# Moving the key stores of later scans, and most loads of values and keys, from SyncE's queue to ScalarE's

## The chip, the cores and the metric

The kernel runs on one core of a Trainium2 chip. The metric is the device time of one execution in microseconds (us); lower is better. Engines are named as in the profile: PE is TensorE's matmul, PEld its weight load, DVE is VectorE, ACT is ScalarE, POOL is GpSimd, and SP is SyncE, which in this kernel issues every DMA. A DMA is issued by an instruction in an engine's queue, which waits there, in order, until what it needs is ready.

## What is computed

A gated linear attention with complex decay per channel (4 batches, 8 heads, 768 tokens, head dimension 48) is followed by a 2-D Fourier transform of the tokens and channels with a norm and two MLP blocks. Cut to what matters:

```python
for t in range(S):                                   # attention, per batch and head
    S_re, S_im = ar*S_re - ai*S_im + outer(k[t], v[t]), ar*S_im + ai*S_re
    y[t] = q[t] @ S_re
x = y as [4, 768, 384]
u = x + real(fft(fft(x, tokens), channels)); un = norm(u)
x = u + relu(un @ w_ch1) @ w_ch2                     # channels 384 -> 1536 -> 384
h = relu(x.T @ w_tok1) @ w_tok2                      # tokens 768 -> 256 -> 768
u = x + h.T
out = u + relu(u @ w_ch1') @ w_ch2'
```

## The kernel before, in words

**A chain and dense work for each batch.** The *chain* of a batch is `stage1` (attention) and `stage2` (the Fourier transform as matmuls, and the norm). The *dense work* is the MLPs: `dense1`/`mlp2` and at the end `mlp`, whose long groups of matmuls are L934 (first product, nine matmuls 128x384 into a PSUM tile `l`) and L956 (second product, also nine); ACT evicts the first product with L938 into `h` (for some batches also L944 into `full`), DVE makes the remainder L947 from it, and DVE adds the second product at L959. There are three `l` tiles in PSUM. The chain of batch b+1 is laid over the dense work of batch b: the matmuls of a chain have priority on PE and dense work fills the gaps. On ACT, DVE, POOL and SP the priorities are the other way round (dense 0, conversion of weights 5, chain 10). A scheduler turns these priorities and its own estimates into one fixed order for each engine, so that a changed instruction moves others as well.

**stage1** is a scan of each channel's decay in steps of three tokens, and then a loop over eight chunks of 96 tokens. Batch 0 has its own scan (`first_scan`, stores at L452). Batches 1 to 3 use `scan`: of each of 16 steps, `st_a` loads (L554, L558), `st_b` to `st_f` make the decays on ACT, DVE and POOL, `st_g` makes two tiles `y` on DVE (L634, L637; four buffers `y00`, `y10`, `y01`, `y11`, named by tile and by the step's parity) and stores one half of each to `kn` in DRAM (L638, L639), and `st_t` transposes the tile on PE (L650, tile `s`) and copies it on ACT into `qkt` (L653, L655, L656). In the profile these stores are `kn<-y`. The two `kn` arrays of batches b and b+1 alternate.

**The loop over chunks** needs for chunk c the values `V` (one load, L749) and the keys `Kn` (two loads, L752, from `kn`). Both have two buffers; the loads of chunk c+2 stand behind the matmuls that read those of chunk c (L776, L777 and for V also L810, L816). ACT evicts the chunk's result into `xT` (L818), and DVE carries a state `T` from chunk to chunk.

**Conversions.** The weights come as pairs of 32-bit words and are converted once, under batches 0 and 1: a load `cvt` (L185, 56 of them), ACT L191 and L192, DVE L194, POOL L196, DVE L199, ACT L205, POOL L206, and a store to `wscr` (L207). All later uses load `w<-wscr` (L283, 180 of them). All of these DMAs are on SP's queue, and a DMA that waits holds up those behind it:

```python
        def load(self):
            ...
            w = self.place(p, j, b)
            sp.dma_start(out=r32(w), in_=wscr[p][j])
```

Of the kernel before, what the change touches and what calls it, by code (L numbers as in the profile page):

```python
# [48 lines left out]
def with_ap(ap, offset, dims):  # L49
    return bass.AP(ap.tensor, ap.offset + offset, [list(ap.ap[0])] + [list(d) for d in dims])  # L50
# [3 lines left out]
def attn_fft_mixer_kernel(ctx: ExitStack, tc: tile.TileContext, aL, xL, vL, wL, qN, kN, vN, arN, aiN,  # L54
# [18 lines left out]
    ve, se, ge = Prio(nc.vector, "v"), Prio(nc.scalar, "v"), Prio(nc.gpsimd, "v")  # L73
    te, sp = Prio(nc.tensor, "pe"), Prio(nc.sync, "sp")
# [17 lines left out]
    def alloc(tag, shape, dt=F32, name=None):  # L92
        n = 1
        for x in shape[1:]:
            n *= x
        t = pool.tile([128, SIZE[tag]], dt, tag=tag, bufs=BUFS[tag], name=name or tag)
        return shaped(t[0:shape[0], 0:n], shape)
# [3 lines left out]
    def palloc(tag, shape):  # L101
        n = 1
        for s in shape[1:]:
            n *= s
        t = psum.tile([128, 512], F32, tag=tag, bufs=PSB[tag], name=tag)
        v = t[0:shape[0], 0:n]
        if len(shape) == 3:
            v = v.rearrange("p (a b) -> p a b", b=shape[2])
        return v
# [438 lines left out]
    def scan(b, t, knd, qk):  # L548
# [78 lines left out]
        def st_g(i):  # L627
            d = t[i]
            m, P, xx, s0 = d["m"], d["P"], d["xx"], d["s0"]
            y1, y2 = ybuf[0][i % 2], ybuf[1][i % 2]  # L630
            x1 = xx[:, :, 0, :].unsqueeze(2).to_broadcast([128, m, 2, 48])
            o1 = with_ap(y1, 0, [(128, m), (64, 2), (1, 48)])
            o2 = with_ap(y2, 0, [(128, m), (64, 2), (1, 48)])
            ve.tensor_tensor(out=o1, in0=x1, in1=P[:, 0:m, 0:2, :], op=ALU.mult)  # L634
            ve.tensor_tensor(out=xx[:, :, 1, :], in0=xx[:, :, 1, :], in1=P[:, 0:m, 2, :], op=ALU.mult)
            x2 = xx[:, :, 1, :].unsqueeze(2).to_broadcast([128, m, 2, 48])
            ve.tensor_tensor(out=o2, in0=x2, in1=P[:, 0:m, 0:2, :], op=ALU.mult)  # L637
            sp.dma_start(out=knd[0, :, s0:s0 + m, :], in_=y1[0:64, 0:m, :])  # L638
            sp.dma_start(out=knd[1, :, s0:s0 + m, :], in_=y2[64:128, 0:m, :])  # L639

        def st_t(i, k):
            if not qk:
                qk.append(alloc("qk", [112, 12288], name="qkt").rearrange("p (k g s) -> p k g s", k=2, g=64))
            qkt = qk[0]
            d = t[i]
            s0 = d["s0"]
            y = ybuf[k][i % 2]
            ps = palloc("s", [112, NT, 128])
            for j in range(NT):
                te.transpose(ps[:, j, :], y[:, j, 0:112], ident)  # L650
            src = ps.rearrange("p s (g c) -> p g c s", g=2)
            if k == 0:
                se.copy(out=with_ap(qkt, s0, [(64 * 96 + 48, 2), (96, 64), (1, NT)]), in_=src)  # L653
            else:
                se.copy(out=with_ap(qkt, 64 * 96 + 47 - s0, [(96, 64), (-1, NT)]), in_=src[:, 0])  # L655
                se.copy(out=qkt[:, 0, :, 48 + s0:48 + NT + s0], in_=src[:, 1])  # L656

        def st_end():

            ends = alloc("e", [128, 2, 3, 48], name="ends")  # L660
            for j, f in enumerate((t[15]["P"][:, NT - 1], t[16]["P"][:, 0])):
                se.copy(out=ends[:, j], in_=f)
            t[0]["ends"] = ends
            F = ends[:, 1]
            w = alloc("e", [128, 2, 48], name="len")
            ve.tensor_tensor(out=w, in0=F[:, 0:2], in1=F[:, 0:2], op=ALU.mult)
            ve.tensor_tensor(out=w[:, 0], in0=w[:, 0], in1=w[:, 1], op=ALU.add)
            ve.tensor_tensor(out=w[:, 0], in0=w[:, 0], in1=F[:, 2], op=ALU.mult)
            se.activation(out=w[:, 1], in_=w[:, 0], func=ACTF.Square, scale=-1.0, bias=ones, accum_out=chk[:, 0:1])
            ve.tensor_reduce(out=chk[:, 1:2], in_=F[:, 2], axis=mybir.AxisListType.X, op=ALU.add)  # L670
            ve.tensor_scalar(out=good, in0=chk[:, 1:2], scalar1=CHK_C, scalar2=None, op0=ALU.is_lt)
            ve.scalar_tensor_tensor(out=good, in0=chk[:, 0:1], scalar=CHK_B, in1=good, op0=ALU.is_lt, op1=ALU.mult)
# [19 lines left out]
        for i in range(NS):  # L692
            if i + ahead < NS:
                st_a(i + ahead)
            n = t[i]["n"]
            for j in range(5):
                if j == 2:
                    part2(i + 1)
                if j == 4:
                    part1(i + 2)  # L700
                if j < n:
                    st_f(i, j)
            if t[i]["m"]:
                st_g(i)
                st_t(i, 0)
                st_t(i, 1)
        st_end()

    def stage1(b):
        t = [dict() for _ in SL]  # L710
        knd = kn[b % 2]
        qk = []
        tops = free if b == 0 else []
        if b == 0:
            first_scan(t, knd, qk)
        else:
            scan(b, t, knd, qk)
# [28 lines left out]

        def ch_load(c):
            v = alloc("P", [96, 384], name="V")
            sp.dma_start(out=v, in_=vL[b, c])  # L749
            kt = alloc("A", [96, 8, 128], name="Kn")  # L750
            for hf in range(2):
                sp.dma_start(out=kt[48 * hf:48 * hf + 48],  # L752
                             in_=knd[hf].rearrange("(h c) s f -> c s h f", c=8)[c])
            st[c] = dict(v=v, kt=kt)

# [64 lines left out]
        if b == 0:  # L820
            tick(CF[0])
        st_g2()
        ch_load(0)
        ch_load(1)
        ch_sc(0, 0)
        ch_sc(0, 1)
        for c in range(8):
            if c < 7:
                ch_u(c)
                ch_sc(c + 1, 0)  # L830
                ch_sc(c + 1, 1)
            ch_y(c)
            if b == 0 and WC[c]:
                warm(WC[c], ident)
            st["T"] = st.get("Tn")
            if c < 6:
                ch_load(c + 2)
            if b == 0 and c < 7:
                rests[0], rests[1] = tops[c], st["yop"]
                tick(CF[c + 1], c == 5)  # L840
# [520 lines left out]
```

## Time and profile before

| | |
|---|---|
| time, median of 3 runs | 1092.18 us (1091.67 to 1096.09) |
| the profiled execution | 1093.5 us, of which the trace's span is 1091.7 |
| busy: PE, PEld, DVE, ACT, POOL | 978.8, 915.3, 769.3, 511.1, 417.9 us |
| mean granted clock of PE | 0.966 |
| scans (first to last store) of batches 1, 2, 3 | 194.5 to 340.6; 422 to 522; 603 to 722 us |
| loops over chunks of batches 0 to 3 | 77 to 136; 344 to 397; 524 to 578; 723 to 776 us |

Busy time is the time in which an engine executed something; issuing a DMA is not counted in it. The spans of scans and loops are read from the starts of the stores, loads and matmuls named above. The end of the chain of batch 3 lies at about 831 us; after 850 us only dense work is left.

### The profile page before, as it was taken

How to read it: one execution, taken by the hardware profiler on the slowest of the kernel's cores; microseconds unless marked ns; L12 is line 12 of the kernel's file. 1: busy time of each engine (PE TensorE's matmuls, PEld its weight loads, DVE VectorE, ACT ScalarE, POOL GpSimd, SP SyncE). 2: the span in 40 equal slices, each digit the busy share in tenths (PEclk: the TensorE clock that was granted, in tenths of full speed). 3: DMA queues.
4: the chain of work that ended last, by engine and by line, in shares of the span. 5: the costliest groups of instructions: out<-in, count | busy, mean ns of one | idle time of the engine just before them, and what ended most of it. 6: DMA issues, size and time to landing. Idle time of an engine off the chain costs nothing.

```text
span 1091.7 us, 21067 instructions
## 1 busy us (share of the span) xinstructions
PE 978.8 (90%) x7314; PEld 915.3 (84%) x7314; DVE 769.3 (70%) x2083; ACT 511.1 (47%) x1425; POOL 417.9 (38%) x541
## 2 busy tenths in 40 slices
PE   1567788999899988999998999999897999999997
PEld 0337766989788986899997899999787999999997
DVE  6988887999999678999658879974734433433332
ACT  6753446777875236877216556842224112121111
POOL 6625994673676454345336312424512002000000
PEclk9988896999999999899999999999998999999999
DMA  6238943776668563465575345665303434543432
GB/s 219 48 101 233 290 165 118 252 264 206 200 235 270 162 180 113 117 184 175 156 198 148 100 139 187 203 165 132 128 17 117 146 114 135 159 156 127 163 101 76
DMA packets 101537, 174.66 MB, mean 160 GB/s; under 512 B 11056, under 2 KB 61104, under 8 KB 100912
## 3 DMA queue, kind: packets, MB, share of 16 engines
q1 hardware_dynamic: 101424, 173.24, 51.5%
q8 instruction: 60, 0.98, 0.4%
q14 instruction: 53, 0.43, 0.1%
HBM read 133.88 MB, written 39.32 MB: 159 GB/s over the span
## 4 chain that ended last, share of the span: by engine, by line
PE 68%; DVE 16%; DMA 6%; POOL 4%; ACT 3%; issue 2%; SPq 0%; POOLq 0%; DVEq 0%; ACTq 0%
PE l L956 24%; PE l L934 23%; PE s L761 4%; DMA cvt<-wL 3%; PE s L650 2%; PE s L1047 2%; PE s L810 2%; DVE cvt L199 2%; DVE ws L1002 2%; PE s L1036 1%; PE s L816 1%; PE s L1161 1%; POOL cvt L196 1%; DVE ws L996 1%; PE s L1179 1%
## 5 line engine op out<-in xcount | busy, mean ns | idle before, releaser
L956 PE MATMUL l<-w,h 128*128 128x384 f32 x1728 | 326.5, 339 | 6.8 <-DVE h L947 4.0
L934 PE MATMUL l<-th,w 128*128 128x384 f32 x1152 | 316.0, 344 | 8.8 <-DVE h L947 4.3
L956 PEld LDWEIGHTS l<-w,h 128*128 128x128 f32 x1728 | 297.2, 188 | 11.1 <-DVE h L947 6.3
L934 PEld LDWEIGHTS l<-th,w 128*128 128x128 f32 x1152 | 213.1, 191 | 12.2 <-DVE h L947 6.1
L934 PE MATMUL l<-tl,w 128*128 128x384 f32 x576 | 196.3, 341 | 3.6 <-DVE tl L918 3.6
L938 ACT ACTIVATE h<-l 128x384 fp32r<-128x384 f32 x192 | 94.1, 490 | 213.2 <-PE l L934 212.7
L959 DVE TENSOR_TENSOR u<-u,l 128x384 f32<-128x384 f32 x192 | 105.3, 549 | 83.1 <-PE l L956 82.4
L947 DVE SCALAR_TENSOR_TENSOR h<-l,h 128x384 fp32r<-128x384 f32 x160 | 88.5, 553 | 91.0 <-ACT h L938 90.8
L934 PEld LDWEIGHTS l<-tl,w 128*128 128x128 f32 x576 | 110.3, 191 | 4.2 <-DVE tl L918 4.2
L196 POOL TENSOR_TENSOR cvt<-cvt 128x384 int32<-128x384 int32 x56 | 66.3, 1190 | 38.3 <-DVE cvt L194 7.3
L761 PE MATMUL s<-qkt 112*96 112x96 f32 x512 | 57.8, 263 | 11.0 <-DVE sc L768 11.0
L472 PE MATMUL s<-misc,y 128*112 128x128 f32 x96 | 22.2, 379 | 47.3 <-DVE y L450 44.5
L761 PEld LDWEIGHTS s<-qkt 112*96 112x96 f32 x512 | 51.8, 173 | 13.8 <-DVE sc L768 12.0
L472 PEld LDWEIGHTS s<-misc,y 128*112 128x112 f32 x96 | 14.8, 183 | 57.0 <-POOL tm L366 19.1
L1146 POOL TENSOR_TENSOR xl<-u,xh 128x384 fp32r<-128x384 f32 x18 | 17.9, 1005 | 107.1 <-ACT xh L1145 107.1
L206 POOL TENSOR_TENSOR w<-cvt,w 128x384 fp32r<-128x384 f32 x44 | 52.2, 1197 | 8.3 <-ACT w L205 8.0
L199 DVE SCALAR_TENSOR_TENSOR cvt<-cvt 128x384 int32<-128x384 int32 x56 | 45.9, 828 | 5.9 <-POOL cvt L196 5.8
L579 POOL TENSOR_TENSOR tm<-tm 128x144 f32<-128x144 f32 (+1 forms) x51 | 26.8, 526 | 58.9 <-ACT tm L578 58.6
L945 POOL TENSOR_TENSOR h<-full,h 128x384 fp32r<-128x384 f32 x32 | 33.8, 1057 | 37.2 <-ACT full L944 35.4
L623 DVE TENSOR_TENSOR p<-p,A 128x144 f32<-128x144 f32 x144 | 44.6, 310 | 2.1
L650 PE MATMUL s<-misc,y 128*112 128x128 f32 x288 | 45.2, 276 | 0.9 <-DVE y L634 0.3
L794 POOL TENSOR_TENSOR yc<-Aa,gm 48x384 f32<-48x384 f32 x18 | 21.0, 1164 | 62.4 <-DVE Aa L787 62.4
(232 smaller groups left out, 1940.8 us busy)
## 6 DMA issues: line engine op xcount, KB each, us to landing
w<-wscr SPq DMA_DIRECT2D x180, 384.0 KB, 3.4
cvt<-wL SPq DMA_DIRECT2D x56, 384.0 KB, 5.0
wscr<-w SPq DMA_DIRECT2D x44, 384.0 KB, 3.7
Kn<-kn SPq DMA_DIRECT2D x64, 192.0 KB, 3.7
kn<-y SPq DMA_DIRECT2D x96, 96.0 KB, 2.6
raw<-aL SPq DMA_DIRECT2D x48, 144.0 KB, 3.1
xx<-xL SPq DMA_DIRECT2D x48, 144.0 KB, 2.9
V<-vL SPq DMA_DIRECT2D x32, 144.0 KB, 3.2
```

What stands on the lines that cost most here:

```text
L196: x = ge.tensor_tensor(out=a, in0=a, in1=lo, op=ALU.add)
L199: rest(ve.scalar_tensor_tensor(out=a, in0=hi, scalar=-0x80000000, in1=a, op0=ALU.bitwise_and, op1=ALU.bitwise_or))
L206: ge.tensor_tensor(out=parts[:, 1, :], in0=a.bitcast(F32), in1=r32(parts[:, 0, :]), op=ALU.subtract)
L472: te.transpose(ps[:, j, :], y[:, j, 0:112], ident)
L623: ve.tensor_tensor(out=cur, in0=prev, in1=A[:, j, 0:3, :], op=ALU.mult)
L650: te.transpose(ps[:, j, :], y[:, j, 0:112], ident)
L761: te.matmul(out=ps[:, j, :], lhsT=K[:, hc, :], rhs=Q[:, hc, :])
L934: te.matmul(out=ps, lhsT=w1[:, wi, kt * 128:kt * 128 + 128], rhs=x[g][:, kt, :], start=(n == 0), stop=(n == 8))
L938: x = se.activation(out=hi, in_=ps, func=ACTF.Relu)
L947: ve.scalar_tensor_tensor(out=lo, in0=ps, scalar=0.0, in1=r32(hi), op0=ALU.max, op1=ALU.subtract)
L956: te.matmul(out=ps, lhsT=hs[m][:, hi, tt * 128:tt * 128 + 128], rhs=w2[:, wi, :], start=(n == 0), stop=(n == 8))
L959: ve.tensor_tensor(out=u[tt], in0=u[tt], in1=ps, op=ALU.add)
```

## The change

The two stores of a scan's step leave `st_g` and SP's queue; in `st_t` each is written behind the copies of its tile, on ACT's queue. Of the loads of `V` and `Kn` those of chunks 0 and 1 stay on SP; those of chunks 2 to 7 go to ACT's queue. This holds for all four batches, whereas the stores of batch 0's scan (L452) stay. So 96 stores, 24 loads of `V` and 48 of `Kn` change the queue; no byte more or less is moved.

```diff
@@ scan.st_g
             ve.tensor_tensor(out=o2, in0=x2, in1=P[:, 0:m, 0:2, :], op=ALU.mult)
-            sp.dma_start(out=knd[0, :, s0:s0 + m, :], in_=y1[0:64, 0:m, :])
-            sp.dma_start(out=knd[1, :, s0:s0 + m, :], in_=y2[64:128, 0:m, :])
@@ scan.st_t
                 se.copy(out=with_ap(qkt, 64 * 96 + 47 - s0, [(96, 64), (-1, NT)]), in_=src[:, 0])
                 se.copy(out=qkt[:, 0, :, 48 + s0:48 + NT + s0], in_=src[:, 1])
+            h = slice(64 * k, 64 * k + 64)
+            se.dma_start(out=knd[k, :, s0:s0 + d["m"], :], in_=y[h, 0:d["m"], :])
@@ ch_load
             v = alloc("P", [96, 384], name="V")
-            sp.dma_start(out=v, in_=vL[b, c])
+            q = se if c > 1 else sp
+            q.dma_start(out=v, in_=vL[b, c])
             kt = alloc("A", [96, 8, 128], name="Kn")
             for hf in range(2):
-                sp.dma_start(out=kt[48 * hf:48 * hf + 48],
+                q.dma_start(out=kt[48 * hf:48 * hf + 48],
                              in_=knd[hf].rearrange("(h c) s f -> c s h f", c=8)[c])
```

In the kernel after, lines behind `ch_load`'s new line are higher by one (L939 is the old L938), `ch_load`'s are L750 and L753, the stores are L656, and the copies L651, L653 and L654.

On SP, in the loop over chunks of batch 0, the order before is:

```order
L752 DMA Kn_957<-kn0_101 48x8x128 x2
L749 DMA V_955<-vL 96x384
L185 DMA cvt_962<-wL 128x768
L185 DMA cvt_966<-wL 128x768
L752 DMA Kn_1029<-kn0_101 48x8x128 x2
L749 DMA V_1027<-vL 96x384
L185 DMA cvt_1038<-wL 128x768
L185 DMA cvt_1042<-wL 128x768
L752 DMA Kn_1105<-kn0_101 48x8x128 x2
L207 DMA wscr00_104<-w_1108 128x768
L749 DMA V_1103<-vL 96x384
```

And after:

```order
L753 DMA Kn_886<-kn0_101 48x8x128
L753 DMA Kn_891<-kn0_101 48x8x128
L185 DMA cvt_962<-wL 128x768
L185 DMA cvt_966<-wL 128x768
L185 DMA cvt_1038<-wL 128x768
L185 DMA cvt_1042<-wL 128x768
L207 DMA wscr00_104<-w_1108 128x768
L185 DMA cvt_1122<-wL 128x768
L185 DMA cvt_1126<-wL 128x768
L207 DMA wscr01_105<-w_1112 128x768
```

The loads of V and Kn are gone from between the conversions' loads L185, which now follow each other, ahead of the stores L207.

On ACT, in the scan of batch 2, near the same dense product (`l_6858`), the order before is:

```order
L655 COPY qkt_5238<-s_5499 112x64x3
L656 COPY qkt_5238<-s_5499 112x64x3
L586 ACTIVATE tm_5531<-tm_5531 128x144
L600 ACTIVATE A_5570<-tm_5531 128x3x48
L938 ACTIVATE h_6857<-l_6858 128x384
L944 ACTIVATE full_6869<-l_6858 128x384
L598 COPY A_5570<-A_5570 128x3x48
L566 ACTIVATE sq_5583<-raw_5454 128x288
L601 ACTIVATE A_5570<-A_5570 128x3x48
L938 ACTIVATE h_6857<-l_6872 128x384
L653 COPY qkt_5238<-s_5545 112x2x64x3
L944 ACTIVATE full_6883<-l_6872 128x384
```

And after:

```order
L578 ACTIVATE tm_5531<-tm_5531 128x144
L656 DMA kn0_101<-y00_69 64x384
L586 ACTIVATE tm_5531<-tm_5531 128x144
L939 ACTIVATE h_6857<-l_6858 128x384
L945 ACTIVATE full_6869<-l_6858 128x384
L656 DMA kn0_101<-y10_71 64x384
L600 ACTIVATE A_5570<-tm_5531 128x3x48
L566 ACTIVATE sq_5583<-raw_5454 128x288
L601 ACTIVATE A_5570<-A_5570 128x3x48
L598 COPY A_5570<-A_5570 128x3x48
L939 ACTIVATE h_6857<-l_6872 128x384
L651 COPY qkt_5236<-s_5543 112x2x64x3
```

The stores of this step (`y00`, `y10`) stand ahead of the copies of its tiles into `qkt`, not behind them as the code writes it: the first ahead of the eviction of `l_6858`, the second between it and the eviction of `l_6872`.

On PE, in `stage2` of batch 3, before (L1047 and L1094 are the chain's, L956 is dense; each row is a group of matmuls of one tile):

```order
L1047 MATMUL s_9591<-ws_9502 128x193 x4
L956 MATMUL l_10333<-w_10258,h_10262 128x384 x3
L956 MATMUL l_10333<-w_10291,h_10295 128x384 x3
L956 MATMUL l_10344<-w_10166,h_10229 128x384 x3
L1094 MATMUL s_9599<-misc_64,xT_87 128x112 x4
L956 MATMUL l_10344<-w_10258,h_10262 128x384
L1094 MATMUL s_9608<-misc_64,ws_9502 128x112 x4
L956 MATMUL l_10344<-w_10258,h_10262 128x384 x2
L956 MATMUL l_10344<-w_10291,h_10295 128x384 x3
L1047 MATMUL s_9626<-ws_9502 128x193 x8
```

And after:

```order
L1048 MATMUL s_9591<-ws_9502 128x193 x4
L1095 MATMUL s_9599<-misc_64,xT_87 128x112 x4
L957 MATMUL l_10377<-w_10166,h_10229 128x384
L957 MATMUL l_10377<-w_10258,h_10262 128x384 x2
L1095 MATMUL s_9608<-misc_64,ws_9502 128x112 x4
L957 MATMUL l_10377<-w_10258,h_10262 128x384
L957 MATMUL l_10377<-w_10291,h_10295 128x384 x3
L1048 MATMUL s_9626<-ws_9502 128x193 x8
L1095 MATMUL s_9638<-misc_64,xT_87 128x112 x4
L1095 MATMUL s_9647<-misc_64,ws_9502 128x112 x4
L1048 MATMUL s_9665<-ws_9502 128x193 x3
```

The tile `l_10377` is the last product of the dense work that is ordered under this chain. Counted along PE's order, 2070 dense matmuls (of L934, L956, L1161 and L1179) stand ahead of the transposes of the sixteenth step of batch 3's scan before, and 2097 after; ahead of the first L1047 of batch 3 they are 2277, and 2304 after; ahead of the first L914 behind that chain they are 2304 in both. In batch 1's chain the last L1036 and all behind it have the same 936 in both.

## Rows read from the trace of the kernel before

**Rows 1.** Part 1 of the page: busy time, share, instructions.
```profile
PE 978.8 (90%) x7314; PEld 915.3 (84%) x7314; DVE 769.3 (70%) x2083; ACT 511.1 (47%) x1425; POOL 417.9 (38%) x541
```

**Rows 2.** Part 4 of the page: the chain that ended last, by engine.
```profile
PE 68%; DVE 16%; DMA 6%; POOL 4%; ACT 3%; issue 2%; SPq 0%; POOLq 0%; DVEq 0%; ACTq 0%
```

**Rows 3.** The windows view, in stretches of 50 us and the tail.
```profile
core 0: us, PE busy (x) PEld busy (x) DVE busy (x) ACT busy (x) POOL busy (x), PEclk, DMA share, GB/s
100.00:150.00 50.00, 37.96 (x437) 33.49 (x437) 45.70 (x70) 21.90 (x52) 46.18 (x37) 0.90 0.82 259
750.00:800.00 50.00, 46.42 (x524) 43.41 (x519) 30.04 (x43) 12.55 (x33) 23.07 (x18) 0.97 0.38 113
800.00:850.00 50.00, 43.08 (x248) 38.69 (x247) 22.98 (x62) 15.73 (x36) 8.82 (x12) 0.93 0.26 81
850.00:1050.00 200.00, 200.00 (x1167) 199.74 (x1166) 76.39 (x139) 36.06 (x75) 6.07 (x6) 1.00 0.42 139
```

**Rows 4.** The windows view: three scans, and the last loop over chunks.
```profile
205.00:340.00 135.00, 124.83 (x723) 117.28 (x722) 129.42 (x375) 102.76 (x289) 83.76 (x109) 1.00 0.70 233
444.00:522.00 78.00, 78.00 (x473) 77.04 (x472) 72.45 (x248) 61.67 (x195) 37.35 (x64) 0.98 0.57 167
646.00:722.00 76.00, 76.00 (x466) 75.26 (x465) 69.66 (x239) 55.13 (x171) 27.54 (x52) 1.00 0.62 191
723.00:768.00 45.00, 45.00 (x612) 42.50 (x610) 23.86 (x60) 9.86 (x24) 14.52 (x14) 1.00 0.56 143
```

**Rows 5.** The waits of SP's queue: line, cause, us, times, longest us.
```profile
SPq L638 <- DVE xx L635: 61.0, 29, 7.7
...
SPq L749 <- PE s L816: 35.0, 14, 4.1
```

**Rows 6.** The waits of PE and ACT for loads, whole kernel.
```profile
PE l L776 <- DMA Kn<-kn: 0.6, 1, 0.6
PE l L776 <- DMA V<-vL: 0.5, 1, 0.5
...
ACT cvt L191 <- DMA cvt<-wL: 14.1, 13, 3.8
```

**Rows 7.** The source view of the moved DMAs: ns min/median/max, starts.
```profile
L639 SPq DMA_DIRECT2D kn<-y x48: 445/451/1577, 195.4 to 722.3; - x48
...
L749 SPq DMA_DIRECT2D V<-vL x32: 316/336/606, 8.5 to 767.6; - x32
...
L752 SPq DMA_DIRECT2D Kn<-kn x64: 302/430/1338, 76.6 to 763.2; - x64
```

**Rows 8.** The source view of the stores, 444 to 522 us.
```profile
L638 SPq DMA_DIRECT2D kn<-y x14: 445/451/452, 444.9 to 521.1; - x14
...
L639 SPq DMA_DIRECT2D kn<-y x13: 445/451/452, 446.0 to 517.4; - x13
```

**Rows 9.** Dense evictions, 444 to 522 us: groups by line, then waits.
```profile
L938 ACT ACTIVATE h<-l 128x384 fp32r<-128x384 f32 x24 | 12.0, 498 | 3.3 <-PE l L934 3.3
...
ACT h L938 <- PE l L934: 3.3, 6, 0.7
...
DVE h L947 <- ACT h L938: 0.9, 1, 0.9
```

**Rows 10.** The timeline of SP's queue, of ACT and POOL, batch 0's chunks.
```profile
85.05 0.82 SPq L752 DMA_DIRECT2D Kn<-kn  x2
...
89.61 1.25 SPq L185 DMA_DIRECT2D cvt<-wL  x2
...
93.62 0.56 ACT L191 ACTIVATE cvt<-cvt 128x384 f32<-128x384 f32 x1 [3.79 <-DMA cvt<-wL]
...
96.93 1.37 POOL L206 TENSOR_TENSOR w<-cvt,w 128x384 fp32r<-128x384 f32 x1 [2.25 <-ACT w L205]
```

**Rows 11.** The waits of ACT, 85 to 120 us.
```profile
ACT cvt L191 <- DMA cvt<-wL: 6.9, 5, 3.8
```

## The prediction

> **What bounds the kernel now.** First the page's busy times: PE executes for 978.8 us of a span of 1091.7, and ACT for 511.1 [rows 1]. The chain that ended last is PE for 68% of the span, DVE 16%, DMA 6%, ACT 3%, and SP's queue 0% [rows 2]. So the time is PE's work plus PE's gaps, and the question is which gaps the change can open or close. The windows view answers that: behind 850 us PE is busy in all of 200 us (1167 matmuls, so 0.171 us each), and no chain is left there. Gaps lie earlier: 12.0 us of PE between 100 and 150 us, under a DVE at 45.7 and a POOL at 46.2 of 50, and again 3.6 and 6.9 us between 750 and 850 us [rows 3], where the last chain ends. There the dense work that may fill gaps runs out in both kernels: 2304 dense matmuls stand ahead of the first L914 behind the chain. While dense work lasts, a delay of a chain costs nothing at once. It is paid at 750 to 850 us, when the chain has more left to do and fewer matmuls beside it.
>
> Next the stretches that the change enters. In the scans of batches 2 and 3 PE is full (78.00 of 78.00 and 76.00 of 76.00), DVE is at 72.45 and 69.66, ACT at 61.67 and 55.13. In batch 1's scan DVE is the full one, 129.42 of 135. In the last loop over chunks ACT does 9.86 us in 45, with PE full [rows 4].
>
> Last the waits. SP's queue waits 61.0 us at the stores L638 alone, for DVE, and 35.0 at the loads L749 for the chunk's matmuls [rows 5]. Whoever needs a DMA behind them hardly notices: PE waits 0.6 and 0.5 us for Kn and V, and only the conversion's L191 loses anything, 14.1 us in 13 waits for its loads [rows 6]. SP's long waits are no cost in themselves.
>
> **The change part by part.** *Issue time that moves.* A store takes SP 0.451 us, a load of V 0.336 and one of Kn 0.430 (medians) [rows 7]. So ACT gets 96 x 0.451 + 24 x 0.336 + 48 x 0.430 = 43.3 + 8.1 + 20.6 = 72.0 us, if it issues as slowly as SP. No row of this trace shows a DMA issued by ACT. The nearest rows are SP's, with which I work; the lower bound is nothing, because issuing might lie beside an ACTIVATE that runs.
>
> *Loads on ACT in the loops over chunks: 0.* In a loop there are 6 x 0.336 + 12 x 0.430 = 7.2 us of issue. In the last loop ACT does 9.86 us of 45 [rows 4], which leaves 35 us of cover; the other loops have room as well (batch 0 has it least). The order puts each load just ahead of or behind the eviction L818 of the same products, so that the wait is one ACT would have anyway. Were the cover gone, three loops would cost 21.5 us; I see nothing that takes it, and leave it to the slower rival.
>
> *Stores on ACT in the scans: +4.6, bounds 0 and +43.3.* In 78 us of batch 2's scan there are 14 + 13 = 27 stores [rows 8], 12.2 us of issue. ACT goes from 61.67 to 73.9 us of 78; the idle time falls from 16.3 to 4.1. The 24 evictions L938 of dense products in that stretch waited for PE only 6 times, so 18 found their product lying ready: ACT was often late already, and DVE waited for it 0.9 us [rows 9]. The order puts the stores ahead of the copies of their own step, where each waits straight for DVE's `y`, and behind a store stand evictions of dense products; if these are late, PE runs out of its three `l` tiles. This much can be lost: nothing (the tiles absorb it, as they do before), or the issue of every store, 43.3 us. Between these I go by how the chain falls behind. In the order after, 27 more dense matmuls stand ahead of batch 3's last scan step (2097 against 2070) and of its first L1047 (2304 against 2277). At 0.171 us each [rows 3] the chain is 27 x 0.171 = 4.6 us later with PE full, and that much cover is missing behind 750 us, where PE has gaps already. It is near the lower bound because PE waited for nothing in the scans, and because the chain needs ACT's copies only for its loop over chunks.
>
> *SP's queue without these waits: -3, bounds 0 and -15.2.* In batch 0's loop the load of Kn went out at 85.05 us and the conversions' loads only at 89.61, behind a load of V that waited for its buffer; L191 then started at 93.62 after 3.79 us of idle time for that load, and POOL's L206 at 96.93 after 2.25 [rows 10]. From 85 to 120 us ACT's waits for conversion loads sum to 6.9 us [rows 11]. In the order after, these loads stand one behind another on SP, ahead of everything that waits for chunks. All waits of ACT and PE for such loads are 14.1 + 0.6 + 0.5 = 15.2 us [rows 6], the upper bound. I take a little under half of the 6.9: DVE is busy for 45.7 of 50 us in that stretch [rows 3] and an earlier load takes nothing from DVE's work. In batch 1's scan DVE is at 96% [rows 4] and I take nothing. The transfers are the same, and the wait for V and Kn is now ACT's.
>
> *Sum.* The profiled execution takes 1093.5 us (1091.7 of span and 1.8 around it), 1.3 above the median of 1092.18. Change: +4.6 - 3.0 + 0 = +1.6, so 1095.1 for such an execution and **1093.8, say 1094, for the median**. By the bounds alone the sum could be anything from -15 to +43.
>
> **A rule against the change.** SP's waits of 61.0 us and the waits of 0.5 and 0.6 us that came of them [rows 5, 6] are weighed above. The Trainium skill, page "DMA: Bandwidth & Descriptors", section "Issuing engines are not separate DMA queues", says that DMAs issued from several engines end up on the same 16 DMA engines, and that issuing them from more than one saves only the sequencer's time to start them, usually small beside the transfer. By that rule taken alone the -3 would be 0 and the sum +4.6, that is 1096.8. The trace agrees for V and Kn, whose users hardly wait; against it stand the 3.79 us at 93.62, a wait not for the transfer but for a place in SP's queue.
>
> **The rivals.** *Slower: ACT becomes the bound of dense work in the scans.* For it: 73.9 us of 78, 18 of 24 products already waiting, and stores that wait for DVE (2.1 us on average, 61.0 in 29, as SP saw it [rows 5]) ahead of evictions. Against it: the three tiles, PE without a wait before, and batch 3's scan, which with as many stores comes to 55.13 + 12.2 = 67.3 of 76. If one scan's worth of stores is exposed, 32 x 0.451 = 14.4 us, the result is 1092.2 + 14.4 - 3 = **1104**. It decides when PE's waits for `l` tiles in batch 2's scan exceed about 8 us.
>
> *Faster: SP was what delayed the conversions.* For it: the 14.1 us of L191, and PE's 12.0 us of gaps between 100 and 150 us. Against it: DVE and POOL nearly full there. If half of 15.2 us comes back, and ACT's stores cost nothing, 1092.2 - 7.6 = **1085**.
>
> *Nothing on ACT: issuing costs it no time.* Then only the -3 stands, if the reordering costs nothing either: **1089**, within what cannot be told from no change. Against it: SP itself needs 0.451 us for a store.
>
> **How the numbers follow.** A measurement of this kernel tells a change of some 0.5%, 5.5 us, from none. The forecast (1094, its own range 1088 to 1098) gets 0.32, the slower rival 0.31, the faster one 0.27, and free issue 0.10. Faster by over 0.5% is the faster rival, 0.27; within 0.5% the forecast and free issue, 0.42; slower 0.31. The range leaves out the far parts of both rivals, a tenth on each side: from 1082, the faster rival with 3 us more of the 15.2 given back, to 1107, the slower one with 7 more stores exposed (7 x 0.451 = 3.2 us).
>
> **What would show it.** Right: ACT's busy time in batch 2's scan unchanged but its idle time down to some 4 us; more waits of PE for L938's evictions there, but under 5 us; PE's gaps between 750 and 850 us up from 10.5 to about 15; the conversions' loads of batch 0's loop issued before 89 us, and L191's 6.9 us nearly gone. Wrong on the slow side: PE waits for ACT or for DVE's L947 in the scans of batches 2 and 3, or SP's loads w wait for DMAs issued by ACT. Wrong on the fast side: PE's gaps between 100 and 200 us shrink by more than 5 us, or the last chain ends before 826 us (831 now).

## The result, and the profile after

The changed kernel takes 1100.47 us (median of 7 runs, 1098.39 to 1105.37) against 1094.86 for the kernel before (7 runs, 1091.67 to 1096.71): a ratio of 1.0067, 95% interval 1.0043 to 1.0092, so some 5 to 10 us slower. The forecast said 1094 from 1092.18, which is +1.8 us; of the 8.3 us from 1092.18 to 1100.47, 2.7 are the kernel before itself, whose median over more runs is 1094.86. The time lies inside the range (1082 to 1107), above the forecast's own range (1088 to 1098), and 3.5 us under the slower rival.

Parts 1 and 4 of the page after; they answer to [rows 1, 2]:

```profile
PE 984.2 (90%) x7314; PEld 918.8 (84%) x7314; DVE 767.3 (70%) x2083; ACT 512.3 (47%) x1425; POOL 416.7 (38%) x541
...
PE 63%; DVE 20%; POOL 6%; issue 4%; DMA 4%; ACT 3%; SPq 0%; DVEq 0%; POOLq 0%; ACTq 0%
```

PE has the same 7314 matmuls and is busy 5.4 us longer, the span is 5.4 us longer (1097.1 against 1091.7), and its idle time is the same: 1097.1 - 984.2 = 112.9 and 1091.7 - 978.8 = 112.9. It would be wrong to read from this that no gap was opened. PE's mean granted clock is 0.966 in the profiled execution before and 0.958 in the one after. In 98 later executions of the kernel before, its median is 0.959, and it reaches 0.966 in only two. Two runs that are described below compare at like clocks. Both issue all 168 DMAs on ACT; `e8` has the order of instructions of the kernel before (clock 0.958, span 1093.3), `e12` that of the changed kernel (0.957, 1098.8). Part 1 of their pages, e8 and then e12:

```profile
PE 985.4 (90%) x7314; PEld 922.2 (84%) x7314; DVE 769.3 (70%) x2083; ACT 511.5 (47%) x1425; POOL 417.6 (38%) x541
...
PE 985.3 (90%) x7314; PEld 920.6 (84%) x7314; DVE 767.7 (70%) x2083; ACT 512.5 (47%) x1425; POOL 416.6 (38%) x541
```

Here PE's work is the same, and its idle time is 107.9 us in e8 and 113.5 in e12. The control `e7`, which has the old order and the old queues, has 106.6 at a clock of 0.957. So the new order does open gaps, some 5 us of them. To see where, the span is cut where the sixth copy `th` of each set ends on ACT (L917, after L918), which closes a chain or the first half of a batch's dense work. The windows view of the kernel before, in these stretches (columns as in [rows 3]):

```profile
0.00:180.10 180.10, 111.35 (x956) 85.81 (x957) 148.29 (x409) 97.83 (x268) 116.19 (x143) 0.89 0.55 169
180.10:290.20 110.10, 103.40 (x589) 97.89 (x590) 100.87 (x301) 84.35 (x243) 64.17 (x88) 0.98 0.70 227
290.20:443.50 153.30, 136.63 (x1217) 124.02 (x1216) 128.74 (x339) 83.22 (x231) 82.42 (x97) 0.97 0.60 185
443.50:579.20 135.70, 135.70 (x1234) 130.51 (x1233) 107.62 (x328) 76.10 (x229) 56.95 (x84) 0.99 0.59 169
579.20:636.90 57.70, 53.09 (x322) 48.55 (x322) 48.90 (x139) 33.70 (x104) 23.69 (x35) 0.97 0.41 120
636.90:832.00 195.10, 184.60 (x1531) 174.98 (x1530) 139.71 (x399) 90.49 (x261) 68.40 (x91) 0.98 0.46 138
```

And of the changed kernel:

```profile
0.00:180.30 180.30, 113.53 (x956) 86.66 (x956) 143.92 (x409) 97.92 (x268) 117.92 (x143) 0.88 0.54 169
180.30:289.50 109.20, 104.49 (x593) 97.71 (x594) 103.48 (x304) 85.27 (x246) 63.42 (x89) 0.99 0.71 228
289.50:447.50 158.00, 138.26 (x1213) 126.38 (x1212) 126.44 (x337) 85.18 (x235) 82.65 (x99) 0.94 0.59 181
447.50:577.80 130.30, 130.30 (x1179) 126.22 (x1179) 104.39 (x321) 71.97 (x218) 54.84 (x81) 0.99 0.60 170
577.80:644.10 66.30, 63.13 (x414) 58.45 (x411) 54.05 (x148) 36.50 (x109) 24.10 (x35) 0.95 0.38 115
644.10:837.10 193.00, 180.26 (x1499) 169.68 (x1499) 139.84 (x395) 90.08 (x261) 67.67 (x91) 0.97 0.48 139
```

The third stretch, from the end of the first half of batch 0's dense work to the end of batch 1's chain, is 4.7 us longer with practically the same matmuls: PE's idle time rises from 16.7 to 19.7 us, and its work takes 1.6 us more at a clock of 0.94 instead of 0.97. Between e8 and e12 it grows by 3.1 us, from 153.8 to 156.9, with 137.71 and 137.44 us of work, so by idle time alone. The last three stretches together are 389.6 against 388.5 us, +1.1, since what the fourth saves the fifth spends (other dense work stands in them); between e8 and e12 they grow by 1.8. The first two are 0.7 us shorter. From first to last store the scan of batch 2 takes 104.9 us instead of 100.1, but its start lies beside batch 1's norm; behind the end of batch 1's chain it takes 79.6 us instead of 78.6. Batch 3's takes 120.1 instead of 119.1. In the stretches of these scans in which PE is full before [rows 4], it is full after as well.

Of the signs that the prediction named, the conversions' loads of batch 0's loop leave from 81.17 us on instead of 89.61, and PE's gaps between 750 and 850 us grow from 10.5 to 12.7 us instead of 15. A sign of its slow side came once: a load `w` on SP waited 12.2 us for loads of `Kn` that ACT issues (by the waits view), but PE waited for no `w`. The waits of ACT for loads, whole kernel, answer to [rows 6]; the wait at L191 falls from 14.1 to 7.5 us, and new waits for `Kn`, 17.7 us together, stand in ACT's own queue:

```profile
ACT h L939 <- DMA Kn<-kn: 10.7, 3, 4.0
...
ACT cvt L191 <- DMA cvt<-wL: 7.5, 10, 1.7
ACT xT L819 <- DMA Kn<-kn: 3.7, 1, 3.7
...
ACT R L1168 <- DMA Kn<-kn: 3.3, 1, 3.3
```

The timeline of ACT in batch 2's scan shows what a store costs there:

```profile
453.30 0.38 ACT L653 COPY qkt<-s 112x192 f32<-112x192 f32 x1
453.43 0.45 ACTq L656 DMA_DIRECT2D kn<-y  x1
453.52 0.31 ACT L598 COPY A<-A 128x144 f32<-128x144 f32 x1
453.92 0.39 ACT L654 COPY qkt<-s 112x192 f32<-112x192 f32 x1
```

The issue takes 0.45 us, as on SP. It runs beside the copy L653, which was under way, and beside L598, which starts 0.09 us after the issue began. What comes next is late: L654 starts at 453.92, 0.04 us after the issue's end and 0.40 us after L598, where in the kernel before an activity started 0.22 us after an L598 (433.10 and 433.32 in the timeline that follows). Of the 96 stores in this trace, 55 are followed by an activity that starts within 0.07 us of the issue's end. So ACT does pay for an issue, as far as nothing that is already under way covers it, and there is room for that: from 449 to 527 us its activities and its 27 issues together cover 64.2 of 78 us, with 7.7 of the 12.4 us of issue beside activities. That leaves 13.8 us idle, not the 4 that the prediction looked for. Of this there was no row before.

Where the third stretch loses, batch 1's norm has to pass through ACT among the first instructions of batch 2's scan. The timeline of ACT before (rs is the norm's scale in three groups of two tiles; the second group's here; L1126 uses the groups' results):

```profile
432.78 0.30 ACT L1115 ACTIVATE rs<-mv,lnc 128x2 f32<-128x2 f32 x1 [1.56 <-DVE mv L1107]
433.10 0.31 ACT L598 COPY A<-A 128x144 f32<-128x144 f32 x1
433.32 0.20 ACT L1116 ACTIVATE rs<-rs 128x2 f32<-128x2 f32 x1
```

And after, with the same two instructions as L1116 and L1117:

```profile
436.01 0.31 ACT L600 ACTIVATE A<-tm 128x144 f32<-128x144 f32 x1
436.22 0.28 ACT L1116 ACTIVATE rs<-mv,lnc 128x2 f32<-128x2 f32 x1
436.41 1.29 ACT L1127 ACTIVATE ws<-u,rs 128x384 f32<-128x384 f32 x2
437.61 0.31 ACT L578 ACTIVATE tm<-tm 128x144 f32<-128x144 f32 x1
437.82 0.31 ACT L601 ACTIVATE A<-A 128x144 f32<-128x144 f32 x1
438.03 0.19 ACT L1117 ACTIVATE rs<-rs 128x2 f32<-128x2 f32 x1
```

Between the pair there are now L1127 twice, L578 and L601: 1.81 us from start to start instead of 0.54, and the first of the pair itself starts 3.4 us later, because on DVE too scan instructions stand ahead. None of these instructions was changed, and no DMA stands here; the two stores ahead of them (430.91 and 432.64 us) were issued while ACT had nothing to run.

### The profile page after: what moved, and what is told of

Its sections match the earlier page's. It is cut to its first block, busy times and chain, and to the rows that moved or that the text cites. A ratio compares the mean times of both kernels' runs of the same rounds, so it can differ in the third digit from the quotient of the medians.

```text
span 1097.1 us, 21076 instructions
## 1 busy us (share of the span) xinstructions
PE 984.2 (90%) x7314; PEld 918.8 (84%) x7314; DVE 767.3 (70%) x2083; ACT 512.3 (47%) x1425; POOL 416.7 (38%) x541
## 4 chain that ended last, share of the span: by engine, by line
PE 63%; DVE 20%; POOL 6%; issue 4%; DMA 4%; ACT 3%; SPq 0%; DVEq 0%; POOLq 0%; ACTq 0%
PE l L957 22%; PE l L935 21%; PE s L762 3%; PE s L648 2%; POOL cvt L196 2%; DMA cvt<-wL 2%; PE s L1048 2%; DVE cvt L199 2%; PE s L811 2%; PE s L1037 2%; DVE ws L1003 1%; PE s L817 1%; PE s L1162 1%; DVE u L960 1%; DVE ws L997 1%
## 5 line engine op out<-in xcount | busy, mean ns | idle before, releaser
L957 PEld LDWEIGHTS l<-w,h 128*128 128x128 f32 x1728 | 301.1, 190 | 11.3 <-DVE h L948 8.4
L939 ACT ACTIVATE h<-l 128x384 fp32r<-128x384 f32 x192 | 94.0, 491 | 214.2 <-PE l L935 201.5
L948 DVE SCALAR_TENSOR_TENSOR h<-l,h 128x384 fp32r<-128x384 f32 x160 | 88.3, 553 | 88.2 <-ACT h L939 87.7
L472 PE MATMUL s<-misc,y 128*112 128x128 f32 x96 | 22.1, 375 | 46.2 <-DVE y L450 43.0
L819 ACT ACTIVATE xT<-s,gate 112x384 f32<-112x384 f32 x24 | 13.9, 580 | 73.2 <-PE s L817 61.3
```

The costliest lines, as they stand in the source:

```text
L939: x = se.activation(out=hi, in_=ps, func=ACTF.Relu)
L948: ve.scalar_tensor_tensor(out=lo, in0=ps, scalar=0.0, in1=r32(hi), op0=ALU.max, op1=ALU.subtract)
L957: te.matmul(out=ps, lhsT=hs[m][:, hi, tt * 128:tt * 128 + 128], rhs=w2[:, wi, :], start=(n == 0), stop=(n == 8))
```

## The experiments

Ratios are to the kernel before, run beside them. "Order" is the sequence of instructions on an engine.

**Halves.** `e1_stores_only` keeps the change in `scan` and takes that of `ch_load` back; `e2_loads_only` does the reverse; `e3_late_sp` moves the stores in the code but not to another queue; `e4_loads_b0` moves the loads of batch 0 alone:

```diff
 e1:  -            q = se if c > 1 else sp
      +            q = sp
 e3:  -            se.dma_start(out=knd[k, :, s0:s0 + d["m"], :], in_=y[h, 0:d["m"], :])
      +            sp.dma_start(out=knd[k, :, s0:s0 + d["m"], :], in_=y[h, 0:d["m"], :])
 e4:  -            q = se if c > 1 else sp
      +            q = se if c > 1 and b == 0 else sp
```

> Only the 96 key stores of the later scans are issued on ScalarE; all loads of values and keys stay on SyncE. Theory A (issuing on ScalarE takes its time and delays the chains): this half alone gives most of the loss, +4 to +7 us over the kernel before, and the later scans become longer. Theory B (the issue is absorbed; what costs is the new order of instructions in batch 1's stage 2, where four stores stand among the chain's copies, and the lower clock of PE behind the gap there): +2 to +6 us, scans as long as before (80 and 86 us within 1 us), all of the loss in the stretch from 397 us to the end of batch 1's chain. Theory C (the loss comes from the loads): no change, within 2 us.

> Only the loads of values and keys of chunks 2 to 7 are issued on ScalarE; the key stores stay on SyncE. Theory A (issue time on ScalarE in the scans): -1 to -3 us, since only the gain of the conversions' loads is left. Theory B (new order in batch 1's stage 2 because of the stores there): -3 to +1 us. Theory C (the loss comes from the loads: ScalarE waits in its queue for a buffer of keys, and evictions stand behind it): +4 to +6 us, with ScalarE waiting over 8 us for keys.

> The key stores are written behind the copies, as in the change, but stay on SyncE, as all loads do: the order on PE and ScalarE changes a little, no queue does. Theory A (issue time on ScalarE): within 2 us of the kernel before. Theory B (any new order can move the end of a chain by some us): a difference of 1 to 4 us of either sign, told by the end of batch 1's chain and PE's clock there. Theory C: within 2 us.

> Only the loads of values and keys of batch 0 (chunks 2 to 7) are issued on ScalarE, everything else as before. The prediction's gain: the conversions' loads leave earlier, 3 us faster, with the chain of batch 0 ending about 3 us earlier. Theory B (an earlier end of the loop is taken back by POOL and by PE's lower clock in batch 0's stage 2, as in the changed kernel, whose loop ended 2.6 us earlier and whose chain ended no earlier): within 1.5 us of the kernel before. Theory C (loads cost): +1 to +3 us.

Measured: e1 1.0047 [1.0031, 1.0063], e2 1.0040 [1.0024, 1.0056], e3 0.9996 [0.9980, 1.0011], e4 0.9982 [0.9965, 0.9999]. Either half alone costs 4 to 5 us and both together about 7, so they do not add. That speaks against a price for each DMA. e1's time fits theories A and B alike, and not all of its loss lies where B put it: its last three stretches take 391.7 us against 388.5. e2 has theory C's time, but C's mechanism does not explain it: ACT waits 3.8 and 3.4 us for `Kn` in it, in one wait each, less than in the changed kernel, and e8 below has 30.7 us of such waits and no loss. Its last three stretches take 392.4 us. e4 was to be the prediction's gain: -2 us [-3.8, -0.1], where -3 was expected. In its one trace ACT waits for conversions' loads only 1.3 us between 85 and 120 us, but the chain of batch 0 ends at 181.6 us, no earlier than in the kernel before (180.1) or in e7 (181.0), so where the 2 us come from is not shown. The stretch of batch 1 is 156.5 us in e1, 155.5 in e2 and e3, and 153.4 in e4. e3 is no slower than the kernel before, so 2 us of this stretch in one trace prove nothing by themselves.

**Queue or order.** The order of the four computing engines was written into the kernel, as edges that fix the order only and wait for nothing. `e5_new_queues_old_order` is the changed kernel with the order of the one before; `e6_old_queues_new_order` the reverse; `e7_swapped_stores` exchanges L638 and L639 as a control:

```diff
 e5, e6:
+        for a, z in zip(o, o[1:]):
+            tc.add_manual_dep(made[e][z], made[e][a].name, HOLD, reason="order")
 e7:
-            sp.dma_start(out=knd[0, :, s0:s0 + m, :], in_=y1[0:64, 0:m, :])
             sp.dma_start(out=knd[1, :, s0:s0 + m, :], in_=y2[64:128, 0:m, :])
+            sp.dma_start(out=knd[0, :, s0:s0 + m, :], in_=y1[0:64, 0:m, :])
```

> All 168 DMAs are issued on ScalarE as in the changed kernel, but the instructions of PE, ScalarE, VectorE and GpSimd stand in exactly the order of the kernel before. Theory A (issuing on ScalarE takes its time and delays what stands behind): +4 to +7 us over the kernel before, like the changed kernel. Theory B (the loss is the new order that the scheduler made of the change): within 2 us of the kernel before, or up to 3 us faster from the conversions' earlier loads.

> All DMAs are issued on SyncE as in the kernel before, but the instructions of PE, ScalarE, VectorE and GpSimd stand in exactly the order of the changed kernel. Theory A (issue on ScalarE): within 2 us of the kernel before. Theory B (new order): +4 to +7 us, with the last chain's end at about 836 us against 831, and 27 dense matmuls fewer left behind the sixteenth step of batch 3's scan.

> The two stores of a step on SyncE's queue change places, and nothing else: PE, ScalarE, VectorE and GpSimd keep the order of the kernel before. All theories: within 1 us of the kernel before. It shows how far a second profile of practically the same program differs: PE's idle time and the time that its work takes at the granted clock, stretch by stretch. If batch 1's stage 2 differs by 2 us or more here, the 4.7 us there are in part a matter of the execution.

Measured: e5 1.0032 [1.0013, 1.0051], e6 1.0099 [1.0075, 1.0123], e7 1.0006 [0.9990, 1.0021]. The new order costs 11 us with every DMA on SP, more than the change itself and more than theory B expected; the new queues cost 3 us with the old order. In neither run was the order of the DMAs on SP held, and both figures contain what that costs. The batch 1 stretch tells them apart, here of e6 and then of the control e7:

```profile
289.00:451.30 162.30, 140.58 (x1216) 128.61 (x1215) 127.31 (x338) 84.92 (x236) 82.46 (x99) 0.93 0.56 177
```

```profile
290.60:444.00 153.40, 139.66 (x1218) 128.22 (x1216) 128.95 (x339) 83.58 (x231) 82.60 (x97) 0.94 0.59 184
```

The old order gives 153.3 to 153.4 us in the kernel before, e4, e5 and e7, at clocks that differ by 0.03 (a second profile's work at 139.66 us beside 136.63, with less idle time), and 153.8 and 154.9 in e8 and e9 below; the new order gives 158.0 and 162.3, and 156.1 and 156.9 in e11 and e12 below. Two waits of PE in e6 (whole kernel) show part of why:

```profile
PE s L914 <- ACT ws L1126: 15.5, 5, 4.7
...
PE s L776 <- DMA Kn<-kn: 4.0, 2, 3.8
```

The second contains one wait of 3.8 us, in the batch 1 stretch, for a load of keys on SP, whose order was not held; the changed kernel has no such wait. The first is the wait behind the norms, 15.7 us in the changed kernel. At the end of batch 1's chain alone, PE waits ahead of its transposes for 9.3 to 9.4 us in every run with the new order (the changed kernel, e6, and e12 below), with the DMAs on ACT or, in e6, on SP. It waits 6.7 us in every run with the old order there (the kernel before, e5, e7, and e8 and e9 below), with the DMAs on SP or on ACT. So these 2.7 us go with the order and not with the queue. In e1, e2, and e11 below, whose orders are others again, the wait is 9.5, 7.5 and 8.9 us.

The 3 us of e5 lay elsewhere: the second stretch, in which most of batch 1's scan lies, became 115.0 us instead of 110.1, with one wait of ACT:

```profile
270.13 0.45 ACTq L656 DMA_DIRECT2D kn<-y  x1
274.83 0.55 ACT L191 ACTIVATE cvt<-cvt 128x384 f32<-128x384 f32 x1 [5.34 <-DMA cvt<-wL]
```

and on SP's timeline the load it waited for, behind three loads of weights:

```profile
265.00 0.36 SPq L558 DMA_DIRECT2D xx<-xL  x1
267.57 1.36 SPq L283 DMA_DIRECT2D w<-wscr  x3
268.98 2.39 SPq L185 DMA_DIRECT2D cvt<-wL  x2
```

In the kernel before, this load left at 264.80, ahead of them. SP's order had not been held in e5.

**Everything held.** `e8_new_queues_all_pinned` also holds the order of the DMAs that stay on SP; where the 168 moved ones stand among ACT's instructions is left to the scheduler. `e9_new_queues_old_start` holds all orders only up to the end of batch 1's chain. `e10_stores_twice_pinned` is e8 with a second copy of each store, into an array that nothing reads:

```diff
 e10:
             se.dma_start(out=knd[k, :, s0:s0 + d["m"], :], in_=y[h, 0:d["m"], :])
+            se.dma_start(out=kn2[k, :, s0:s0 + d["m"], :], in_=y[h, 0:d["m"], :])
```

> All 168 DMAs are issued on ScalarE; the instructions of PE, ScalarE, VectorE and GpSimd, and now the DMAs that stay on SyncE as well, stand in the order of the kernel before. In the run before this one a load of a conversion stood 4 us later on SyncE and held up batch 1's scan. Theory A (issuing on ScalarE takes its time): +3 us or more. Theory B (only the order costs): within 2 us of the kernel before, all six stretches within 1 us, and the stretch of batch 1's scan back from 115 to about 110 us.

> All 168 DMAs are issued on ScalarE; only the part of the order up to the end of batch 1's chain (about 443 us) is that of the kernel before, the rest is left to the scheduler. Theory B in full (the interleaving of batch 2's scan with batch 1's norm is what costs): within 2 us of the kernel before, the stretch from 290 us to batch 1's end back from 158 to 153 us. Theory B in part (later stretches of the new order cost as well): +2 to +5 us, with batch 1's stretch at 153 and the last chain's end 2 to 5 us late. Theory A: +4 us or more with batch 1's stretch above 155.

> As the run with all orders pinned, and each of the 96 stores is issued on ScalarE a second time, into an unused array: twice the issue on ScalarE in the scans, 43 us more by the rate of SyncE. Theory A: +5 to +15 us over the run with single stores. Theory B (issue is absorbed): within 3 us of it, with PE as full in the scans of batches 2 and 3 as before.

Measured: e8 0.9987 [0.9974, 1.0000], e9 1.0018 [1.0003, 1.0033], e10 1.0293 [1.0272, 1.0313]. With every order held, moving 168 DMAs to ACT's queue costs nothing. Two of e8's six stretches missed the expected 1 us, and they cancel: 178.2 us instead of 180.1 for the first, 112.3 instead of 110.1 for the second. With only the start held, 2 us of loss remain, and from 443 us to the last chain's end e9 takes 391.3 us against 388.5: the later part of the new order costs too. e10 missed both expectations: 96 more issues cost 34 us over e8, 0.36 us each. Two or four stores in a row stand one behind another. The timeline of ACT in e10 (L657 the stores, L658 the second copies):

```profile
471.37 0.60 ACT L652 COPY qkt<-s 112x384 f32<-112x384 f32 x1
472.09 0.45 ACTq L657 DMA_DIRECT2D kn<-y  x1
472.58 0.61 ACTq L658 DMA_DIRECT2D kn<-y  x1
473.28 0.55 ACTq L657 DMA_DIRECT2D kn<-y  x1
473.88 0.61 ACTq L658 DMA_DIRECT2D kn<-y  x1
474.53 0.31 ACT L599 COPY A<-A 128x144 f32<-128x144 f32 x1 [2.56 <-DVE yt L625]
```

Batch 2's scan takes 87 us here (464 to 551 us) and 78 in e8 (445 to 523), and PE waits there for ACT's `full`, which its waits list as 4.0 us in 3 (L947, the old L944):

```profile
464.00:551.00 87.00, 80.31 (x471) 75.04 (x471) 71.64 (x244) 60.62 (x194) 37.05 (x64) 1.00 0.61 178
```

```profile
PE l L937 <- ACT full L947: 4.0, 3, 2.6
```

ACT's work and its 26 + 26 issues (medians 0.453 and 0.607 us) sum to 60.62 + 27.6 = 88.2 us of 87. Part of them overlap, though: together they cover 76.1 us, and 66.0 of 78 in e8. So ACT is not full (10.9 us are left idle, 12.0 in e8); the 10.1 us that are added come in where the scan waits for them, and it is 9 us longer. Here the slower rival's mechanism is at work.

**The norm alone.** `e12_changed_pinned` is the changed kernel with its own order on all five engines written down, as a control. `e11_norm_first` differs from it only in batch 1's norm between 430 and 445 us; on ACT:

```diff
 L575 ACTIVATE tm<-tm,lnc
+L1116 ACTIVATE rs<-mv,lnc
+L1117 ACTIVATE rs<-rs
 L598 COPY A<-A
 ...
 L600 ACTIVATE A<-tm
-L1116 ACTIVATE rs<-mv,lnc
 L1127 ACTIVATE ws<-u_3204,rs
 ...
-L1117 ACTIVATE rs<-rs
```

> The changed kernel with its own order on all five engines, in which only batch 1's norm is moved ahead of batch 2's scan in one place: some 15 small instructions on VectorE and 6 on ScalarE between 430 and 445 us. Theory B (these stand behind the scan's and hold up the end of batch 1's chain by about 4 us): the end of that chain 2 to 4 us earlier than in the changed kernel, the time 2 to 4 us less than that of the next run. If only PE's clock or what lies ahead of 430 us costs: within 1 us of it.

> The changed kernel with its own order on all five engines written down, as the control of the run before: +4 to +7 us over the kernel before, as the changed kernel, by every theory. The stretch from 290 us to the end of batch 1's chain again near 158 us (theory B), or nearer to 154 if the 4.8 us there were a matter of that one execution.

Measured: e11 1.0027 [1.0013, 1.0042], e12 1.0055 [1.0031, 1.0079]; the medians are 1097.53 and 1101.07 us. The medians differ by 3.5 us, as expected. The two intervals overlap, but both kernels were run beside the same runs of the kernel before, and compared with each other (12 runs and 7) their means differ by 3.1 us, 95% interval 0.7 to 5.5. The profiles, one execution of each, show less: the stretch of batch 1 is 156.1 us in e11 and 156.9 in e12. The timeline of PE in e12 (L915 are the transposes that close the chain):

```profile
437.17 1.54 PE L915 MATMUL s<-misc,ws 128*128 128x128 f32 x6 [4.20 <-ACT ws L1127]
443.04 2.18 PE L915 MATMUL s<-misc,ws 128*128 128x128 f32 x9 [4.33 <-ACT ws L1127]
446.09 0.90 PE L915 MATMUL s<-misc,ws 128*128 128x128 f32 x3 [0.87 <-DVE tl L919]
```

and in e11:

```profile
435.18 1.54 PE L915 MATMUL s<-misc,ws 128*128 128x128 f32 x6 [4.25 <-DVE u L1100]
438.35 1.54 PE L915 MATMUL s<-misc,ws 128*128 128x128 f32 x6 [1.63 <-ACT ws L1127]
440.32 0.90 PE L915 MATMUL s<-misc,ws 128*128 128x128 f32 x3 [0.42 <-ACT ws L1127]
443.85 0.90 PE L915 MATMUL s<-misc,ws 128*128 128x128 f32 x3 [2.63 <-DVE tl L919]
```

The second group's transposes come 4.7 us earlier and PE's wait of 4.33 us ahead of them falls to 1.63, which shows that the norm's place held them up. But 2.63 us come back ahead of the last three, behind scan instructions that were left ahead of the copies `th`. So the mechanism is shown and the wait moved on. By the times this one place owns some 3 us of the loss, with the wide interval above.

## Why the prediction was off, step by step

- **What bounds the kernel.** Right: PE's gaps at the ends of chains decide (e12 has 5.6 us more of them than e8), and SP's long waits cost next to nothing (e8, which takes the stores and most of the loads off SP, is 1.4 us faster [-2.8, 0.0]).
- **Loads in the loops over chunks: 0.** Right for the queue (e8). In e2 they cost 4 us; that the new order did this is inferred from e8, since e2 was not run in the old order.
- **Stores in the scans: +4.6.** The issue itself costs the kernel 0, the lower bound, as e8 shows. The prediction added all 12.2 us of issue to ACT's work and came to 4 us of slack; the traces leave 13.8 us (12.0 in e8), because much of it runs beside activities. A second issue of each store does cost (e10). The rest of the term, the chain that falls behind by 27 dense matmuls, is partly borne out: the last chain's stretch has 12.7 us of idle time instead of 10.5, and e9 measures 2 us for a new order behind batch 1 alone.
- **SP's queue without these waits: -3.** Right about the wait, and near in size by e4's time, -2 us, though e4's trace does not show the gain. L191's waits from 85 to 120 us fall from 6.9 us [rows 11] to 1.2. With the old order held on SP as well, batch 0's chain ends at 178.2 us (e8) and 177.6 (e9), against 180.1 before. In the changed kernel the gain is gone by 180 us: batch 0's loop ends 2.6 us earlier, the chain no earlier (180.3), and PE's clock from 160 to 180 us is 0.57 where it was 0.69.
- **The term that was missing: batch 1's stage 2, +4.7.** This is the step that failed: the prediction has no term for the reordering of this chain. The order was read on PE, where batch 1's chain has the same 936 dense matmuls ahead of it before and after. But on DVE and ACT the scan of batch 2 had been drawn in ahead of batch 1's norm. The edit touches neither. The 4.7 us are those of the first two profiles; e8 and e12 give 3.1, and e11 gives 3.1 [0.7, 5.5] for one place in the norm.
- **The sum.** -2 for the loads and about +2 for the later chains, both within the bounds, and +4.7 for the place not looked at come to +4.7; the measured ratio is +7 us [+5, +10], and what makes up the difference is open. That the time lies inside the range is in part luck: slower by over 0.5% had a chance of 0.31, all of it for ACT as the bound of the scans, and that is not what happened.
- **The rivals.** ACT's issues holding up the scans: wrong with one store, right with two. Conversions as the bound: wrong, since a half of 14.1 us of waits at L191 went and the chain did not end sooner in the changed kernel; where it did, in e8 by 1.9 us, the time fell by 1.4. Free issue, 1089: right on its mechanism (e8 is 1.4 us faster than the kernel before, at the edge of its interval), wrong in that the reordering came with it. The rule of the Trainium skill (page "DMA: Bandwidth & Descriptors", section "Issuing engines are not separate DMA queues") that another issuing engine saves only the sequencer's time agrees with e8: 0.9987.

## What to carry to other kernels

Where a scheduler sets the order, an edit is two changes, the one written and the reordering that follows; hold the order of every engine (the DMA queues among them) and measure the written one alone. Read the new order on the engines that a chain passes through at its end, not on PE alone: the same count of matmuls ahead of a chain says nothing of what stands ahead of its norm. A DMA issue on a computing engine delays what stands behind it there, as far as the engine has nothing under way beside it; one can be free for the kernel and a second one behind it not, so a price is asked for the place where it stands. And before the idle times of two profiles are compared, their granted clocks must be alike.

## What the hardware showed that was not expected

An issue of 0.45 us on ACT's queue runs beside the activities already under way, and the activity behind it starts 0.04 us after its end (453.88 and 453.92 us). Issues in a row do not overlap: four take from 472.09 to 474.49 us, ACT sits idle for 2.56 us, and 96 further issues cost 34 us. And a lower granted clock goes with more time of PE at work and less of it idle, while the span hardly moves: the kernel before and e7 differ only in the order of two stores, and have 978.8 us of work and 112.9 of idle time at a mean clock of 0.966, and 986.4 and 106.6 at 0.957, in spans of 1091.7 and 1093.0 us.
